# Window attention into a two-layer FFN on one core: the two blocks of a visit multiplied together, queues tied in written order, second-layer weights decoded from the eighth block on

## The chip, the cores and the metric

The kernel runs on one core of a Trainium2 chip. The metric is device time in microseconds from the first to the last instruction, with what lies around them; several runs are taken, and their median counts. PE is the matrix engine, DVE the vector engine, ACT the scalar engine, POOL the GpSimd engine, SP the queue from which all DMA is issued. TensorE's clock has two levels, 1.2 and 2.4 GHz; a granted clock of 1.00 is the higher one all the time.

## The reference

Three stages in a row, all in fp32:

```python
# attention: q, k, v are (4, 8, 576, 64)
scores = (q @ k^T) / sqrt(64), masked to the 64 last positions (0 <= i - j < 64)
x = softmax(scores) @ v                # as (2304, 512): heads side by side
# first layer: w1, w2, w3 are (512, 768), w_out is (768, 512)
x2 = max(x @ w1, x @ w2, x @ w3) @ w_out
# second layer: w_in is (512, 2048), w_out is (2048, 512)
h = x2 @ w_in
g = where(h >= 1, h, where(h <= -1, 0, (h + 1)**2 / 4))
out = g @ w_out                        # (2304, 512)
```

## The kernel before

Every large product is made of three passes: weights and inputs are split into a high half that the matmul takes and a low remainder (high times high, and the two mixed products). The weights come as 64-bit words and are decoded on the chip, 128 x 512 of them at a time, which the text calls a tile: `w_load` issues the DMA (L142), and `w_split` (L154) works on ACT (L165 and a copy, both in place on `wst`), then DVE (a shift, L169, and an add, L170, into `wt`), then ACT (the high half into the slot) and POOL (the remainder, L111). Four `wst` buffers (`NW`) and two `wt` buffers (`WT`) stand in a ring. The loads of q and k for later blocks (`raw`, L208) use the same `wst` ring.

Attention goes by blocks of 64 queries with a window of 128 keys, 36 blocks in all. The stages of a block g are `load`, `vload`, `prep` (transposes of q and k; on DVE from block 16 on, L261), `qk` (scores into `sps2`, L288, then DVE's masked reductions to the maximum, L293), `ex` (ACT's exponentials, L304), `norm` (DVE and POOL), `ptr` and `ptc` (PE transposes and the ACT copy `pt`) and `pv` (value products into `ops2`, L342, an ACT copy and a DVE subtraction into `xt`). `sps2` and `ops2` each hold two blocks, by g % 2, in the same PSUM banks.

The first layer goes by nine blocks of 256 tokens (`blocks1`). A first-step item (`a_item`, L351) is 12 matmuls of 256 columns for one of three weights and one of six columns; an ACT copy or a DVE maximum into `ht` takes it out of PSUM, and after the third weight ACT and POOL make the two halves of `h`. A second-step item (`b_item`, L380) is 18 matmuls, an ACT copy to `x2s` (two buffers) and a store to DRAM on SP. Products, second-layer products and the transposes of q and k share three PSUM buffers (`pmm`).

The order is written by hand in units: an `a_item` is one unit, a `b_item` 1.5, `begin[j]` is where block j starts, and `put` sets every stage at a position. The second step of a block follows the first six items of the next one (`BD`). From block 8 of the attention on, two blocks are done in one visit, a visit every 12 units (`VISITS`, `VSTEP`): a visit holds the value products of one pair, the transposes of the next pair and the scores of the pair after that. Visits start at unit 18. From there on `chained` (L549) ties PE's instructions in the written order; the instructions of the other engines are ordered by a scheduler, which works at build time.

At the end of the attention (0.1 units ahead of the ninth block: the turn), the attention's memory is closed, and `x2t`, more weight slots (`v0` to `v7`) and accumulators (`pacc`) are opened there. The 32 tiles of the second layer (`order2`: w_in and w_out in turn) go to `v0` to `v7` and then to the first layer's slots `u0` to `u23` as they come free. Four are issued at the turn and two with each step of the first 16 of the second layer; the scheduler may move their steps earlier where buffers allow. The second layer goes by blocks of 512 tokens: `c_mm` (12 matmuls, L541), `c_act` (ACT and DVE), and `d_item` (12 matmuls into four accumulators, L606) three steps behind.

## Time and profile before

| what | value |
|---|---|
| median of 3 runs (lowest, highest) | 863.98 us (861.62, 864.16) |
| the profiled execution: its time, its span | 864.39 us, 862.3 us |
| PE busy, share of the span | 798.3 us, 93% |
| DVE, ACT, POOL busy | 363.9, 356.2, 157.9 us |
| share of PE in the chain that ended last | 77% (DVE 5%, DMA 4%, ACT 4%) |
| mean granted clock | 0.985 |

The profiled execution's 864.39 us are its span and 2.1 us around it; it lies 0.41 us above the median. A busy PE is not PE at its peak, since matmuls are pipelined and their ends are modelled. By place, the program is: attention and first layer under the loading and decoding of the first weights to about 90 us, attention and first layer together to about 395 us, the turn to about 458 us, the second layer to the end.

### The profile page before, as it was taken

The page shows a single profiled execution, that of the slowest core. Times are in us where ns is not written, and L with a number is a line of the kernel's source. Part 1 is how long each engine was busy: PE and PEld are TensorE (multiplying, and loading weights), DVE is VectorE, ACT ScalarE, POOL GpSimd, SP SyncE. Part 2 cuts the span into 40 slices and gives each one's busy share as a digit, 9 for nine tenths or more (in the row PEclk, how much of TensorE's full clock was granted, in tenths as well). Part 3 has the DMA queues.
Part 4 walks back from the last instruction along what each step waited for, and adds up shares of the span by engine and source line. Part 5 has one row for each costly group of instructions (what it writes and reads, how often), then busy time and mean ns, then how long its engine had stood idle before and what let it go on. Part 6 is the DMA issues. An engine that isn't in the chain of part 4 may idle for free.

```text
span 862.3 us, 14835 instructions
## 1 busy us (share of the span) xinstructions
PE 798.3 (93%) x5776; PEld 701.6 (81%) x5776; DVE 363.9 (42%) x937; ACT 356.2 (41%) x871; POOL 157.9 (18%) x157
## 2 busy tenths in 40 slices
PE   6698889999999898999779999999999999999998
PEld 4597778889898888898778888888888888888896
DVE  5778422323333432316678733433343334333343
ACT  6988533333333534324779422322232223222232
POOL 3666311111111121213574200000000000000000
PEclk8899999999999999999989999999999999999999
DMA  9976243233141413003777000100020001000000
GB/s 243 279 216 187 43 84 85 52 70 63 40 80 32 135 26 98 14 26 111 234 222 241 24 1 25 62 0 1 1 74 0 1 1 36 25 1 1 24 26 25
DMA packets 128054, 62.70 MB, mean 73 GB/s; under 512 B 98288, under 2 KB 120816, under 8 KB 127984
## 3 DMA queue, kind: packets, MB, share of 16 engines
q1 hardware_dynamic: 127984, 61.76, 26.2%
q8 instruction: 45, 0.74, 0.4%
q14 instruction: 25, 0.20, 0.1%
HBM read 52.30 MB, written 9.44 MB: 72 GB/s over the span
## 4 chain that ended last, share of the span: by engine, by line
PE 77%; DVE 5%; DMA 4%; ACT 4%; issue 2%; SPq 1%; POOL 1%; DVEq 0%; ACTq 0%; POOLq 0%
PE acc L606 23%; PE hp L541 23%; PE ps L363 18%; PE ps L385 7%; DMA wst<-in_moe_w_in 3%; PE ops L342 2%; PE sps L288 2%; PE pps L324 1%; DVE sm L293 1%; SPq L215 1%; DVE wt L170 1%; DMA x2r<-x_scratch 1%; ACT wst L165 1%; DVE wt L169 1%; ACT wst L108 1%
## 5 line engine op out<-in xcount | busy, mean ns | idle before, releaser
L363 PE MATMUL ps<-xt,u 128*128 128x256 f32 x1944 | 239.1, 283 | 9.1 <-DVE ht L372 4.0
L363 PEld LDWEIGHTS ps<-xt,u 128*128 128x128 f32 x1944 | 232.5, 190 | 13.9 <-DVE ht L372 5.2
L541 PE MATMUL hp<-x2t,u 128*128 128x512 f32 (+1 forms) x720 | 161.6, 372 | 0.0
L606 PE MATMUL acc<-u,g 128*128 128x512 f32 x648 | 160.4, 396 | 0.0
L586 ACT ACTIVATE u<-hp,half 128x512 f32<-128x512 f32 (+1 forms) x80 | 51.5, 644 | 251.6 <-PE hp L541 251.5
L541 PEld LDWEIGHTS hp<-x2t,u 128*128 128x128 f32 x720 | 126.9, 188 | 27.2
L606 PEld LDWEIGHTS acc<-u,g 128*128 128x128 f32 x648 | 120.9, 188 | 28.3
L589 DVE SCALAR_TENSOR_TENSOR gt<-u,hp 128x512 f32<-128x512 f32 (+1 forms) x80 | 50.6, 632 | 165.8 <-ACT u L587 165.7
L372 DVE TENSOR_TENSOR ht<-ps,ht 128x256 f32<-128x256 f32 x108 | 45.4, 421 | 131.3 <-PE ps L363 114.0
L385 PE MATMUL ps<-h,u 128*128 128x256 f32 x648 | 82.8, 287 | 4.8 <-ACT h L108 2.4
L385 PEld LDWEIGHTS ps<-h,u 128*128 128x128 f32 x648 | 79.7, 194 | 7.2 <-ACT h L108 2.6
L111 POOL TENSOR_TENSOR u<-wt,u 128x512 fp32r<-128x512 f32 x48 | 67.5, 1408 | 46.7 <-ACT u L108 44.3
L111 POOL TENSOR_TENSOR h<-ht,h 128x256 fp32r<-128x256 f32 x54 | 42.7, 793 | 129.0 <-ACT h L108 128.7
L315 POOL TENSOR_TENSOR sm<-sm,rs 128x512 f32<-128x512 f32 (+1 forms) x36 | 35.8, 994 | 142.4 <-DVE rs L314 130.3
L304 ACT ACTIVATE sm<-sm,nm 128x128 f32<-128x128 f32 (+1 forms) x144 | 55.2, 388 | 15.2 <-DVE nm L293 15.2
L170 DVE CUSTOM_DVE_ANT_0 wt<-wst,wt 128x1024 uint16<-128x1024 uint16 x56 | 56.2, 1004 | 3.5 <-ACT wst L108 0.6
L108 ACT ACTIVATE h<-ht 128x256 fp32r<-128x256 f32 x54 | 22.3, 414 | 83.7 <-DVE ht L372 83.6
L606 PE MATMUL acc<-v,g 128*128 128x512 f32 x216 | 53.6, 394 | 0.0
L541 PE MATMUL hp<-x2t,v 128*128 128x512 f32 (+1 forms) x240 | 53.5, 371 | 0.0
L593 DVE CAST g<-gt 128x512 fp32r<-128x512 f32 (+1 forms) x80 | 34.2, 428 | 45.5 <-PE acc L606 43.1
L111 DVE TENSOR_TENSOR g<-gt,g 128x512 fp32r<-128x512 f32 (+1 forms) x80 | 51.1, 639 | 2.7
L541 PEld LDWEIGHTS hp<-x2t,v 128*128 128x128 f32 x240 | 41.9, 188 | 8.3
(50 smaller groups left out, 627.6 us busy)
## 6 DMA issues: line engine op xcount, KB each, us to landing
wst<-in_moe_w_out SPq DMA_DIRECT2D x22, 512.0 KB, 4.4
wst<-in_moe_w SPq DMA_DIRECT2D x18, 512.0 KB, 5.7
wst<-in_moe_w_in SPq DMA_DIRECT2D x16, 512.0 KB, 4.3
vr<-in_v SPq DMA_DIRECT2D x24, 256.0 KB, 3.0
x_scratch<-x2s SPq DMA_DIRECT2D x36, 128.0 KB, 1.8
out<-ob SPq DMA_DIRECT2D x18, 256.0 KB, 2.0
x2r<-x_scratch SPq DMA_DIRECT2D x16, 256.0 KB, 2.9
vr<-in_v SPq DMA_DIRECT2D x19, 128.0 KB, 3.4
```

What stands on the lines that cost most here:

```text
L111: eng.tensor_tensor(dst, a, b, op=ALU.subtract)
L170: nc.vector.tensor_tensor(t, t, lo, op=ALU.add)
L304: nc.scalar.activation(sm[:, p, 0:W], sm[:, p, 0:W], AF.Exp, bias=d["nm"][:, p:p + 1], scale=-1.0, accum_out=ss[:, p:p + 1])
L315: nc.gpsimd.tensor_tensor(sm[:, :, 0:W], sm[:, :, 0:W], rs.unsqueeze(2).to_broadcast([P, NP, W]), op=ALU.mult)
L363: nc.tensor.matmul(ps[:, 0:n], w_col((w, f), wl, kt), xt[:, xl, kt, 0:n], start=(x == 0), stop=(x == len(passes) - 1))
L372: nc.vector.tensor_tensor(t[:, 0:n], ps[:, 0:n], part[j, f][:, 0:n], op=ALU.max)
L385: nc.tensor.matmul(ps[:, 0:n], w_col((3, f), wl, dt), hts[j, f][:, xl, 0:n], start=(x == 0), stop=(x == len(passes) - 1))
L541: nc.tensor.matmul(ps[:, 0:n], w_col((4, f), wl, kt), x2t[tb][:, xl, kt, 0:n], start=(x == 0), stop=(x == len(passes) - 1),)
L586: nc.scalar.activation(u[:, 0:n], ps[:, 0:n], AF.Relu, bias=half, scale=2.0 ** (-WS / 2 - 1))
L589: nc.vector.scalar_tensor_tensor(gt[:, 0:n], u[:, 0:n], 2.0 ** WS, ps[:, 0:n], op0=ALU.min, op1=ALU.max)
L593: nc.vector.tensor_copy(g[:, 0, 0:n], gt[:, 0:n])
L606: nc.tensor.matmul(accs[t], g[:, gl, t * P:(t + 1) * P], wslot[5, f][:, wl * 512:(wl + 1) * 512], start=(f == 0 and x == 0), stop=(f == KF ...
```

## The change

In a visit, both blocks' value products stand together, and so do both blocks' scores. `pv` keeps the matmuls alone, and `values` copies and subtracts for two blocks at once; `red` takes the reductions out of `qk` and, like `ex`, goes by two of the four head pairs, at positions of its own (`RED`, `EXP`). The second step of the first block follows two items of the second block instead of six. `chained` ties PE, ACT and DVE, each behind its own last instruction, from the first visit on. The second-layer weights have four slots from the start (`V`); loads and decodes are written as two operations, the first four in the eighth block, 16 more from the turn on 1.8 units apart (`W2STEP`), each decode 4.3 units behind its load, and the last 12 beside the second layer.

```diff
--- before.py
+++ after.py
@@ -46,8 +46,15 @@
 VISITS = (-24, -18, -12)
 VSTEP = 12
 VLEAD = 2
-EXP = (1.1, 2.1)
+RED = (0.3, 2.3)
+EXP = (1.7, 3.7)
 PTC = (0.6, 1.6)
+
+
+EW = 4
+W2STEP = 1.8
+W2LAG = 4.3
+W2IN = 20
 
 
 SEQ = (
@@ -118,6 +125,7 @@
     com = ctx.enter_context(tc.tile_pool(name="com", bufs=1))
     stg = ctx.enter_context(tc.tile_pool(name="stg", bufs=2, reuse_waits="tile"))
     U = [com.tile([P, 1024], F32R, name=f"u{i}") for i in range(NU)]
+    V = [com.tile([P, 1024], F32R, name=f"v{i}") for i in range(EW)]
     ident = com.tile([P, P], F32, name="ident")
     half = com.tile([P, 1], F32, name="half")
 
@@ -288,23 +296,29 @@
                     nc.tensor.matmul(
                         sps2[o:o + BL, bank, g % 2, x, 0:W], d["q"][r, p, :], win(r, p), start=True, stop=True
                     )
-
-        for p in range(NP):
+        d.update(sm=sm, nm=nm, W=W)
+
+    def red(g, pairs=range(NP)):
+        d = st_g[g]
+        _, mask, W = window(g)
+        sm, nm = d["sm"], d["nm"]
+
+        for p in pairs:
             nc.vector.tensor_tensor_reduce(
                 out=sm[:, p, 0:W], in0=sps2[:, p // 2, g % 2, p % 2, 0:W], in1=mask, scale=-QSCALE, scalar=BIG,
                 op0=ALU.add, op1=ALU.min, accum_out=nm[:, p:p + 1],
             )
-        d.update(sm=sm, nm=nm, W=W)
-
-    def ex(g):
+
+    def ex(g, pairs=range(NP)):
         d = st_g[g]
         W, sm = d["W"], d["sm"]
-        ss = apool.tile([P, NP], F32, tag="ss", name="ss", bufs=5)
-        for p in range(NP):
+        if pairs[0] == 0:
+            d["ss"] = apool.tile([P, NP], F32, tag="ss", name="ss", bufs=5)
+        ss = d["ss"]
+        for p in pairs:
             nc.scalar.activation(
                 sm[:, p, 0:W], sm[:, p, 0:W], AF.Exp, bias=d["nm"][:, p:p + 1], scale=-1.0, accum_out=ss[:, p:p + 1]
             )
-        d["ss"] = ss
 
     def norm(g):
         d = st_g[g]
@@ -331,7 +345,7 @@
         act_copy(pt[0:W], d["pps"][0:W])
         d["pt"] = pt
 
-    def pv(g, xt, off):
+    def pv(g):
         d = st_g[g]
         W, pt, vr = d["W"], d["pt"], st_g[max(g, 1)]["vr"]
         ops = ops2[:, g % 2]
@@ -342,8 +356,13 @@
                 nc.tensor.matmul(
                     ops[r, p, :], vr[0:W, 2 * p + h, :], pt[0:W, p, o:o + BL], start=True, stop=True
                 )
-        act_copy(xt[:, 0, :, off:off + BL], ops)
-        sub(nc.vector, xt[:, 1, :, off:off + BL], ops, f32(xt[:, 0, :, off:off + BL]))
+
+    def values(g, n, xt, off):
+
+        o = ops2[:, g % 2:g % 2 + n].rearrange("a g p c -> a p g c")
+        hl = [xt[:, x, :, off:off + n * BL].rearrange("a p (g c) -> a p g c", g=n) for x in range(2)]
+        act_copy(hl[0], o)
+        sub(nc.vector, hl[1], o, f32(hl[0]))
 
 
     xts = {}
@@ -427,11 +446,19 @@
         for o in range(0, n, BL):
             gblock[(t0 + o) // BL] = (j, o)
 
-    def pv_x(g):
+    def val(g, n=1):
         j, o = gblock[g]
         if o == 0:
             xt_new(j)
-        pv(g, xts[j], o)
+        values(g, n, xts[j], o)
+
+    def pv_x(g):
+        pv(g)
+        val(g)
+
+    def qk_r(g):
+        qk(g)
+        red(g)
 
 
     order = []
@@ -465,7 +492,8 @@
     late = b_items(0)
     for j in range(1, len(blocks1)):
         items = first if j == 1 else a_items(j)
-        seq += items[:BD] + late + items[BD:]
+        bd = 2 if j == 1 else BD
+        seq += items[:bd] + late + items[bd:]
         late = b_items(j)
     seq += late
     at, begin = 0.0, {}
@@ -482,8 +510,8 @@
         ptr(g)
         ptc(g)
 
-    stages = (load, vload, prep, qk, ex, norm, ptr_c, pv_x)
-    ops0 = dict(L=load, V=vload, P=prep, Q=qk, E=ex, N=norm, T=ptr_c, X=pv_x)
+    stages = (load, vload, prep, qk_r, ex, norm, ptr_c, pv_x)
+    ops0 = dict(L=load, V=vload, P=prep, Q=qk_r, E=ex, N=norm, T=ptr_c, X=pv_x)
     for x, tok in enumerate(SEQ.split()):
         if tok[0] == "W":
             for _ in range(int(tok[1:] or 1)):
@@ -513,23 +541,31 @@
             put(vt, vload, g)
             put(vq + STAGES[2], prep, g)
             put(vq + 0.02, qk, g)
-            put(vq + EXP[y], ex, g)
-            put(vq + EXP[y] + 1, norm, g)
+            for z in range(2):
+                put(vq + RED[y] + z, red, g, (2 * z, 2 * z + 1))
+                put(vq + EXP[y] + z, ex, g, (2 * z, 2 * z + 1))
+            put(vq + EXP[y] + 2, norm, g)
             put(vt + 0.01, ptr, g)
             put(vt + PTC[y], ptc, g)
-            put(vp, pv_x, g)
-    put(begin[len(blocks1) - 1] - 0.1, None)
+            put(vp, pv, g)
+        put(vp + 0.04, val, g1, 2)
 
     order2 = [(w, f) for f in range(KF2) for w in (4, 5)]
-    slots2, w2n = [], [0]
-
-    def w2_next():
-        n = w2n[0]
-        if n < len(order2):
-            w, f = order2[n]
-            st = w_load((w, f), wi2 if w == 4 else wo2, slots2[n], "col" if w == 4 else "row", f)
-            w_split((w, f), st, nc.gpsimd)
-            w2n[0] += 1
+    slots2, staged = list(V), {}
+
+    def w2_load(n):
+        w, f = order2[n]
+        staged[n] = w_load((w, f), wi2 if w == 4 else wo2, slots2[n], "col" if w == 4 else "row", f)
+
+    def w2_split(n):
+        w_split(order2[n], staged.pop(n), nc.gpsimd)
+
+    turn = begin[len(blocks1) - 1]
+    put(turn - 0.1, None)
+    for n in range(W2IN):
+        at = begin[len(blocks1) - 2] + 1 + 4 * n if n < EW else turn + 0.35 + W2STEP * (n - EW)
+        put(at, w2_load, n)
+        put(at + W2LAG, w2_split, n)
 
     hps = {}
 
@@ -544,36 +580,35 @@
             )
 
     order.sort(key=lambda e: e[:2])
-    tail = [None]
-
-    def chained(fn, *args):
-
-        if tail[0] is None:
+    tails = defaultdict(list)
+
+    def chained(fn, *args, tie=True):
+
+        ends = {}
+        with ExitStack() as stack:
+            for i in [i for e in tails for i in tails[e]] if tie else ():
+                stack.enter_context(tc.issue_after(i))
+            n = len(nc.cur_bb.bb.instructions)
             fn(*args)
-        else:
-            with tc.issue_after(tail[0]):
-                fn(*args)
-        pe = [i for i in nc.cur_bb.bb.instructions[-200:] if i.engine == mybir.EngineType.PE]
-        if pe:
-            tail[0] = pe[-1]
-
+        for i in nc.cur_bb.bb.instructions[n:]:
+            if i.engine in TIED:
+                ends[i.engine] = i
+        for e, i in ends.items():
+            tails[e] = [i] if tie else tails[e] + [i]
+
+    TIED = (mybir.EngineType.PE, mybir.EngineType.Activation, mybir.EngineType.DVE)
     for at, _, fn, args in order:
         if fn:
             if (fn, args) == (b_item, (len(blocks1) - 1, 0)):
-                c_mm(0, 0, pacc, "acc")
-            if at < visits[0]:
-                fn(*args)
-            else:
-                chained(fn, *args)
+                chained(c_mm, 0, 0, pacc, "acc")
+            chained(fn, *args, tie=at >= visits[0])
         else:
             att_stack.close()
             p2 = ctx.enter_context(tc.tile_pool(name="p2", bufs=1, side="right", reuse_waits="tile"))
             pacc = ctx.enter_context(tc.tile_pool(name="pacc", bufs=5, space=PSUM))
-            slots2 += [p2.tile([P, 1024], F32R, name=f"v{i}") for i in range(2 * KF2 - NU)] + U
+            slots2 += [p2.tile([P, 1024], F32R, name=f"v{i}") for i in range(EW, 2 * KF2 - NU)] + U
             for kt in range(KD):
                 x2_split(0, p2, kt)
-            for _ in range(4):
-                w2_next()
     ffn_stack.close()
     gp = ctx.enter_context(tc.tile_pool(name="gp", bufs=1, reuse_waits="tile"))
     gts = {}
@@ -623,8 +658,11 @@
             d_item(*seq[x - DLAG])
         c_act(tb, f)
         if tb == 0:
-            w2_next()
-            w2_next()
+            for n in (2 * f, 2 * f + 1):
+                if W2IN + n < len(order2):
+                    w2_load(W2IN + n)
+                if n >= 2 and W2IN + n - 2 < len(order2):
+                    w2_split(W2IN + n - 2)
         if tb + 1 < len(blocks2):
             pl = gp if (tb + 1) % 2 else p2
             if 8 <= f < 8 + KD:
```

PE in the visit of blocks 16 and 17's scores, before and after, with the semaphores that a row waits for (`ops2` are value products, `pps` transposes, `sps2` scores, the number behind a name is that of its buffer; one row is the first matmul of a group, or the rest of it). Before:

```order
L342 MATMUL ops2_103<-pt_1780,vr_1737 64x64 [waits DMAHW5_49,DMAHW4_49]
L342 MATMUL ops2_103<-pt_1780,vr_1737 64x64 x7
L342 MATMUL ops2_103<-pt_1805,vr_1740 64x64 [waits DMAHW3_49,DVE_49]
L342 MATMUL ops2_103<-pt_1805,vr_1740 64x64 x7
L324 MATMUL pps_2013<-ident_85,sm_1752 128x128 [waits PE_49]
L324 MATMUL pps_2013<-ident_85,sm_1752 128x128 x3
L324 MATMUL pps_2018<-ident_85,sm_1766 128x128 [waits PE_49,Pool_49]
L324 MATMUL pps_2018<-ident_85,sm_1766 128x128 x3
L288 MATMUL sps2_102<-kring_101,qt_1938 64x128 x8
L288 MATMUL sps2_102<-kring_101,qt_1941 64x128 [waits DVE_49]
L288 MATMUL sps2_102<-kring_101,qt_1941 64x128 x7
```

After:

```order
L356 MATMUL ops2_107<-pt_1774,vr_1735 64x64 [waits DMAHW5_49,DMAHW4_49]
L356 MATMUL ops2_107<-pt_1774,vr_1735 64x64 x7
L356 MATMUL ops2_107<-pt_1796,vr_1738 64x64 [waits DMAHW4_49]
L356 MATMUL ops2_107<-pt_1796,vr_1738 64x64 x7
L338 MATMUL pps_2008<-ident_89,sm_1750 128x128 [waits PE_49,Pool_49]
L338 MATMUL pps_2008<-ident_89,sm_1750 128x128 x3
L338 MATMUL pps_2013<-ident_89,sm_1760 128x128 [waits PE_49,Pool_49]
L338 MATMUL pps_2013<-ident_89,sm_1760 128x128 x3
L296 MATMUL sps2_106<-kring_105,qt_1938 64x128 [waits DVE_49]
L296 MATMUL sps2_106<-kring_105,qt_1938 64x128 x7
L296 MATMUL sps2_106<-kring_105,qt_1941 64x128 [waits DVE_49]
L296 MATMUL sps2_106<-kring_105,qt_1941 64x128 x7
```

The matmuls stand in the same places. The second block's value products wait for a DMA alone; the DVE waits at the scores are now those for the transposes of q and k (`prep`), one for each block, which stand about three units earlier in DVE's queue.

ACT in the same visit (`x2s` second step, `xt` values, `pt` the transposes' copy, `sm` exponentials, `ht` and `h` first step). Before:

```order
L108 ACTIVATE x2s<-ps 128x256 x3
L108 ACTIVATE xt<-ops_103 128x4x64 x2
L108 ACTIVATE pt<-pps 128x512 x2
L304 ACTIVATE sm,ss<-sm,nm 128x128 x8
L108 ACTIVATE x2s<-ps 128x256
L108 ACTIVATE ht_2095<-ps 128x256
L108 ACTIVATE h<-ht_2172 128x256
```

After:

```order
L115 ACTIVATE x2s<-ps 128x256 x3
L115 ACTIVATE xt<-ops_107 128x4x128
L115 ACTIVATE x2s<-ps 128x256
L115 ACTIVATE pt<-pps 128x512 x2
L319 ACTIVATE sm,ss<-sm,nm 128x128 x2
L115 ACTIVATE ht_2087<-ps 128x256
L319 ACTIVATE sm,ss<-sm,nm 128x128 x4
L115 ACTIVATE h<-ht_2164 128x256
L319 ACTIVATE sm,ss<-sm,nm 128x128 x2
```

The eight exponentials stood in a row; now they stand in twos and fours, with the copies out of PSUM between them.

ACT in the turn, where the decoded tiles are those of `u3` to `u5` (two rows on one `wst` are the two first steps of a tile, `u` is its last ACT step; `wt_5966` was made from `wst_5964`, and after the change `wt_5603` from `wst_5502`, `wt_5642` from `wst_5544`). Before:

```order
L165 ACTIVATE wst_5964<-wst_5964 128x512
L108 ACTIVATE wst_5964<-wst_5964 128x512
L108 ACTIVATE ht0_5479<-ps_5466 128x256
L108 ACTIVATE u3_64<-wt_5915 128x512
L165 ACTIVATE wst_6006<-wst_6006 128x512
L108 ACTIVATE wst_6006<-wst_6006 128x512
L108 ACTIVATE u4_65<-wt_5957 128x512
L165 ACTIVATE wst_6015<-wst_6015 128x512
L108 ACTIVATE wst_6015<-wst_6015 128x512
L108 ACTIVATE h_5511<-ht1_5509 128x256
L108 ACTIVATE ht0_5527<-ps_5514 128x256
L108 ACTIVATE u5_66<-wt_5966 128x512
```

After:

```order
L173 ACTIVATE wst_5502<-wst_5502 128x512
L115 ACTIVATE wst_5502<-wst_5502 128x512
L115 ACTIVATE u3_64<-wt_5603 128x512
L115 ACTIVATE ht0_5623<-ps_5610 128x256
L173 ACTIVATE wst_5544<-wst_5544 128x512
L115 ACTIVATE wst_5544<-wst_5544 128x512
L115 ACTIVATE u4_65<-wt_5642 128x512
L115 ACTIVATE h_5664<-ht1_5662 128x256
L173 ACTIVATE wst_5583<-wst_5583 128x512
L115 ACTIVATE wst_5583<-wst_5583 128x512
L115 ACTIVATE u5_66<-wt_5669 128x512
```

Before, the last step of a tile stood two tiles behind its first steps; now all three stand in a row, and the first layer's copies stand between whole tiles.

## Rows read from the trace of the kernel before

**Rows 1.** The table by windows of 20 us: the stretch and its length, then busy us (and number) of PE matmuls, PE weight loads, DVE, ACT and POOL, the granted clock as a share of full speed, DMA share and GB/s. A steady stretch of the first layer, the turn to the second layer, and the second layer.

```profile
120.00:140.00 20.00, 18.00 (x196) 17.09 (x195) 6.87 (x31) 7.87 (x27) 4.67 (x6) 1.00 0.45 83
...
440.00:460.00 20.00, 16.52 (x104) 15.51 (x105) 13.19 (x21) 16.05 (x32) 12.47 (x10) 0.83 0.71 221
...
480.00:500.00 20.00, 20.00 (x88) 16.14 (x87) 11.38 (x19) 5.76 (x10) 3.62 (x3) 1.00 0.00 1
```

**Rows 2.** The view of who waited for whom, 100 to 380 us: engine and line, what it waited for, us in total, times, longest.

```profile
PE sps L288 <- DVE nm L293: 12.4, 12, 1.1
PE ops L342 <- DVE xt L111: 12.2, 13, 0.9
```

**Rows 3.** The timeline of one visit (pairs of query blocks), and at its end the last value products before the turn: start us, us, engine, line, operation, out<-in, count [idle before <- what ended it]. Value products are L342, scores L288.

```profile
144.77 0.69 PE L342 MATMUL ops<-pt,vr 128*64 128x64 f32 x16
145.92 0.42 DVE L111 TENSOR_TENSOR xt<-ops,xt 128x256 fp32r<-128x256 f32 x1 [6.86 <-ACT xt L108]
146.40 0.69 PE L342 MATMUL ops<-pt,vr 128*64 128x64 f32 x16 [0.94 <-DVE xt L111]
149.76 0.67 PE L288 MATMUL sps<-kring,qt 64*64 64x128 f32 x16 [1.06 <-DVE nm L293]
...
394.67 0.69 PE L342 MATMUL ops<-pt,vr 128*64 128x64 f32 x16 [0.94 <-DVE xt L111]
```

**Rows 4.** The timelines of PE, ACT and SP over the first three visits, same columns.

```profile
76.97 0.46 PE L288 MATMUL sps<-kring,qt 64*64 64x64 f32 x16 [2.21 <-DVE nm L293]
89.71 0.67 PE L288 MATMUL sps<-kring,qt 64*64 64x128 f32 x16 [1.07 <-DVE nm L293]
102.16 0.68 PE L342 MATMUL ops<-pt,vr 64*64 64x64 f32 x16 [0.94 <-DVE xt L111]
105.52 0.67 PE L288 MATMUL sps<-kring,qt 64*64 64x128 f32 x16 [1.05 <-DVE nm L293]
117.66 1.09 PE L249 MATMUL tp<-ident,nat 128*128 128x128 f32 x8 [2.18 <-ACT x2s L108]
...
117.22 0.38 ACT L108 ACTIVATE x2s<-ps 128x256 f32<-128x256 f32 x1 [5.48 <-DMA x_scratch<-x2s]
...
79.52 3.68 SPq L215 DMA_DIRECT2D raw<-in_q  x7
84.36 13.96 SPq L215 DMA_DIRECT2D raw<-in_q  x25
98.42 5.12 SPq L215 DMA_DIRECT2D raw<-in_k  x11
103.63 1.58 SPq L390 DMA_DIRECT2D x_scratch<-x2s  x1
```

**Rows 5.** The timeline of PE at a stop in the sixth block.

```profile
297.48 2.72 PE L363 MATMUL ps<-xt,u 128*128 128x256 f32 x21 [1.23 <-ACT ht L108]
```

**Rows 6.** The timeline of PE around the turn (L363 first step, L385 second step, L541 and L606 second layer), and of ACT at the copy of the last piece of x2.

```profile
377.55 15.56 PE L363 MATMUL ps<-xt,u 128*128 128x256 f32 x132
...
395.28 5.86 PE L363 MATMUL ps<-xt,u 128*128 128x256 f32 x48
...
448.18 0.80 PE L385 MATMUL ps<-h,u 128*128 128x256 f32 x2 [2.37 <-ACT h L108]
449.37 9.16 PE L385 MATMUL ps<-h,u 128*128 128x256 f32 x55 [0.39 <-POOL h L111]
458.36 8.36 PE L541 MATMUL hp<-x2t,v 128*128 128x512 f32 x36
466.56 2.92 PE L606 MATMUL acc<-v,g 128*128 128x512 f32 x12
...
407.14 0.62 ACT L108 ACTIVATE x2t<-x2r 128x512 fp32r<-128x512 f32 x1
```

**Rows 7.** The chain that ended last, in order of time: start us, us, what; three products of the second step.

```profile
366.05 6.29 PE ps L385 x54
```

**Rows 8.** Part 5 of the page: the exponentials, with busy us, mean ns of one, idle before.

```profile
L304 ACT ACTIVATE sm<-sm,nm 128x128 f32<-128x128 f32 (+1 forms) x144 | 55.2, 388 | 15.2 <-DVE nm L293 15.2
```

**Rows 9.** The timelines of ACT, DVE and POOL in the turn: the decode of second-layer weights (ACT L165, L108 on wst, DVE shift L169 and add L170, ACT copy and POOL remainder to u and v).

```profile
427.84 0.66 ACT L165 ACTIVATE wst<-wst 128x512 f32<-128x512 f32 x1
429.95 0.63 ACT L108 ACTIVATE u<-wt 128x512 fp32r<-128x512 f32 x1 [0.90 <-DVE wt L170]
430.49 0.67 ACT L165 ACTIVATE wst<-wst 128x512 f32<-128x512 f32 x1
...
416.51 1.54 DVE L169 TENSOR_SCALAR wt<-wst 128x512 int32<-128x512 int32 x1 [1.19 <-POOL v L111]
421.02 0.43 DVE L169 TENSOR_SCALAR wt<-wst 128x512 int32<-128x512 int32 x1 [1.18 <-POOL u L111]
421.48 0.69 DVE L170 CUSTOM_DVE_ANT_0 wt<-wst,wt 128x1024 uint16<-128x1024 uint16 x1
428.24 1.68 DVE L170 CUSTOM_DVE_ANT_0 wt<-wst,wt 128x1024 uint16<-128x1024 uint16 x1
...
414.74 3.03 POOL L111 TENSOR_TENSOR v<-wt,v 128x512 fp32r<-128x512 f32 x2
428.01 1.36 POOL L111 TENSOR_TENSOR u<-wt,u 128x512 fp32r<-128x512 f32 x1 [0.60 <-ACT u L108]
...
432.31 0.73 POOL L111 TENSOR_TENSOR h<-ht,h 128x256 fp32r<-128x256 f32 x1
```

## The prediction, as it was made before the changed kernel ran

> **What bounds the kernel now.** I read the busy time by stretch first. In a steady stretch of the first layer PE works 18.00 of 20 us, at the turn from the first layer to the second 16.52 of 20 with a granted clock of 0.83, and in the second layer 20.00 of 20 [rows 1]. So PE is the bound everywhere, the second layer has nothing to give, and what can be won are PE's standing times before about 458 us.
>
> The waits of the first layer come next [rows 2]: PE stood 13 times for DVE at the value products, 12.2 us in all, and 12 times at the scores, 12.4 us. One visit in order of time [rows 3] shows why. The value products of one block run, PE stands 0.94 us until DVE has taken the low half of that block (it starts at 145.92), and only then come the next block's. At the scores PE stands 1.06 us for DVE's reductions. That is 2.0 us a visit, and at 144 to 150 us nothing else holds PE.
>
> Before that, in the first three visits, PE stands 2.21, 1.07, 0.94 and 1.05 us for the same reasons and 2.18 us for an x2s copy; ACT had stood 5.48 us for a store of that tile, because SP issues its stores between long rows of loads of q and k [rows 4]. A smaller loss is 1.23 us at 297.48, for an ACT copy [rows 5], while ACT decodes second-layer weights between its own first-layer work.
>
> The turn [rows 6]: the ninth block's first product starts at 396.7 (the 48 matmuls from 395.28, less one item of 12; 132 matmuls take 15.49 us, so an item is 1.41). The first output product of the second layer starts at 466.56, 69.9 us later. Between them lie 18 items (25.4), 8 second-step products of 2.10 [rows 7] (16.8) and four hidden products (36 matmuls take 8.20, so 4 x 2.73 = 10.9): 53.1 us of work, **16.8 us lost**. Part of that is clock: after 2.37 us of standing, 55 matmuls took 9.16 us [rows 6], where the item's rate gives 6.5.
>
> **The change part by part.**
>
> *Products of a visit together, reductions and copies behind them.* No matmul is added. In the order of the changed kernel the second block's value products and scores no longer wait for DVE's work on the first one. From the fourth visit on that frees 13 waits of 0.94 (12 of the 13 in [rows 2], and that of 394.67 [rows 3]) and 11 of 1.06: **23.6 us**. The two copies to xt become one of double width, as do the subtractions. DVE's first reduction now starts after both blocks' scores, 0.67 us later; nobody waits for it until the next visit's transposes, some 20 us on. I cost that at nothing. The cover that could go is in the PSUM ring of three: a product's buffer must be freed within two items, 2.8 us. The order puts exponentials in twos (2 x 0.39 [rows 8]) between evacuations, so nothing should stand that long. If one exponential per visit stuck out, 13 x 0.39 = 5 us would go; that is the low end, 18.6.
>
> *Tied order from unit 18 and the block-0 second step four items earlier.* In the first visits there are 7.45 us of PE standing [rows 4]. Not all of it can go: stores still stand behind loads of q and k on SP, the first behind 48 raw loads of about 0.45 us instead of 43 (7, 25 and 11 before 103.63 [rows 4]). And the products whose copies need the stores now come four items, 5.6 us, sooner. So ACT stands at the third x2s copy again, and its queue is tied behind it. Against that, the decode of the weights whose buffers the raw loads take over now precedes the first exponentials, which lets the row start some 3 us earlier. I take **3 us**, between -3 and 7.4.
>
> *Decoding no longer slipped early into ACT's queue.* The stop of 1.23 us at 297.48 [rows 5] goes; the four tiles that are now decoded in the eighth block, in buffers of their own, are issued on SP right behind the stores of two blocks before, so their data should be there. **1.2 us**, between -1 and 1.2 (four chains of 2.65 us on ACT stand within the 2.8 us of slack, if nothing else does).
>
> *The turn.* 16 tiles are left in it, each 1.8 units (2.5 us) apart on paper, with 12 more after it. Before, the scheduler interleaved the decodes: on ACT the two first steps of a tile were followed by the last step of an older one, 2.65 us from tile to tile (427.84 to 430.49 [rows 9]). Now the queues are tied in written order and each tile's chain runs alone: two ACT steps, shift and add on DVE, a copy on ACT. The shift alone takes 0.43 us, but 1.54 when POOL is in the previous tile's remainder: it started at 416.51 and ended 0.28 after POOL's row did (417.77) [rows 9]. In the serial chain POOL's 1.36 us always start with the next tile's first step, so the shift ends at about 1.7 us, the add (0.69) at 2.4, the copy (0.63) at 3.0. In five of eleven cycles POOL also has an h part of 0.73; I count half of it. That makes 3.15 us a tile. The fifth tile cannot start before the four pieces of x2 are copied, 10.5 us after the ninth block's start (407.14 [rows 6]). Eleven tiles stand before the last item's h in ACT's queue: 10.5 + 34.7 = 45.2. With h and its POOL part the first of the last four products ends near 47, the others 6.3 later, two hidden products 5.5: the output products start at 58.8 instead of 69.9, with 50.4 us of work (one hidden product less ahead of them). Lost: 8.4 instead of 16.8, so **8.4 us** won. Ends: at 2.65 a tile 13.9 won; with shift 1.54 and add 1.68 [rows 9] in every tile 4.3 a tile, 4 lost.
>
> The Trainium skill, SBUF — State Buffer, section Who interferes with whom, has VectorE and GpSimd share a port pair as an exclusive lock that is held for a whole instruction. By that rule the h part on POOL holds up the add in full, 0.38 us more in five tiles, 2 us in all, and the total would be 830; where the lock also falls on the add in the other tiles, it is the second rival below. The trace bears it out for the shift (ended 0.28 us behind POOL) and for some adds (1.68 beside 0.69), not for all.
>
> The clock was granted at 0.83, a mix of 1.2 and 2.4 GHz, after PE had stood in the turn [rows 1, 6]. My turn still has 8 us of standing, in shorter pieces, and I count no drop; one like the old one costs 2.7 us.
>
> *Sum:* 23.6 + 3 + 1.2 + 8.4 = 36.2 off the profiled execution's 864.39 us, 828.2. That execution lies 0.4 above the median of 863.98, so I say **828 us**. The second layer's start, where DVE and ACT still decode 12 tiles beside the new work, I cost at nothing: at 466 us PE ran there unbroken beside the same decode.
>
> **Rivals.**
>
> *Evacuation stuck behind the visit (slower).* Tied queues put products' evacuations behind the softmax in ACT's queue. If all eight exponentials (3.1 us [rows 8]) stood between a finished product and its free buffer, 13 visits cost 40 us and the kernel ends at 868. It decides from 2.8 us a visit (36.2/13). For it: ACT can no longer be reordered. Against: the order has evacuations between the pairs, and two buffers of slack.
>
> *The turn stays bound by the decode chain.* If POOL holds up shift and add in most tiles, a tile takes 3.7 to 4.3 us, and the turn gives 2 or loses 4: 834 to 840. For it: DVE's long rows beside POOL [rows 9]; and it has no slack, since ACT leads in the turn. Against: POOL is busy in only half of each tile. This is the lock of the page named above.
>
> *The turn is covered.* At 2.65 a tile, with all 7.4 us of the early visits, another 9.9: 818. For it: the shift is short whenever POOL is out of the way.
>
> *The change does not do it.* If the second block's matmuls still waited (both lie in the same PSUM tiles), 23.6 us stay: 851. Against: the order names no wait for DVE there, but for the transposes.
>
> **Numbers.** Forecast 0.58 (822 to 833); turn bound by its chain 0.22; turn covered 0.13; waits stay 0.03; slower 0.04. Leaving out the last two and the tails, the range is 816 to 846. About 0.3%, 2.6 us, can be told from no change. Faster by more than that 0.95, within 0.01, slower 0.04.
>
> **What would show it.** Right: PE busy near 20 of 20 between 130 and 380 us; no wait of value products or scores for DVE; the ninth block's start some 28 us earlier; about 3.1 us from tile to tile on ACT in the turn, PE standing some 8 us. Wrong: new PE waits for ACT's ht or x2s copies in each visit; a turn as long as before; PE standing at the start of the second layer; a first visit later than 118 us.

## The result, and the profile after

The changed kernel took **831.36 us** (median; 830.53 to 832.36) beside 862.8 us of the kernel before in the same comparison: a ratio of 0.964, 95% interval 0.961 to 0.966. Forecast were 828 us and 816 to 846. The profiled execution's span is 830.0 us, against 862.3 before.

The visits first: PE's timeline of one visit, then the stretches by 20 us (columns as in [rows 1]).

```profile
146.22 1.15 PE L356 MATMUL ops<-pt,vr 128*64 128x64 f32 x32
147.30 1.09 PE L338 MATMUL pps<-ident,sm 128*128 128x128 f32 x8
148.32 1.10 PE L296 MATMUL sps<-kring,qt 64*64 64x128 f32 x32
```

```profile
60.00:80.00 20.00, 16.20 (x144) 15.26 (x143) 16.39 (x22) 13.96 (x28) 12.57 (x10) 0.91 0.79 226
80.00:100.00 20.00, 13.34 (x106) 12.14 (x107) 9.21 (x35) 12.01 (x37) 8.17 (x8) 0.83 0.31 57
...
120.00:140.00 20.00, 20.00 (x218) 19.46 (x217) 6.73 (x29) 7.90 (x27) 5.98 (x7) 1.00 0.42 75
...
400.00:420.00 20.00, 16.80 (x125) 15.46 (x124) 9.43 (x17) 11.89 (x24) 9.40 (x9) 1.00 0.47 140
```

The value products of both blocks are one row of 32, and so are the scores; nothing stands in brackets behind them. From 100 to 360 us PE is busy 20.00 of 20 us in every stretch, where it was 15.83 to 19.06, mostly 18.00, and the view of who waited for whom has no row for PE there, where [rows 2] had two of 12 us. What is left lies at both ends: 60 to 100 us, with a clock of 0.91 and 0.83 (before: 0.91 and 1.00), and 380 to 440 us.

Three marks that every kernel here has cut the time into stages: the start of the fourth visit's value products (122.89 before, 126.79 after), the start of the last visit's value products (393.04 and 367.22), and the end.

| us | to the fourth visit | fourth to last visit | last visit to the end | span |
|---|---|---|---|---|
| before | 122.89 | 270.15 | 469.26 | 862.3 |
| after | 126.79 | 240.43 | 462.78 | 830.0 |
| saved | -3.90 | 29.72 | 6.48 | 32.3 |
| forecast | 3 | 23.9 | 9.3 | 36.2 |

The forecast's 23.6, 1.2 and 8.4 are put into the same stages here; one stop of 0.94, that of the last visit, counts in the third. So the sum was nearly right while none of its three parts was: the visits gave more, the start lost where a gain was expected, and the last stage gave less. The experiments take the three apart. The table goes on with them (spans of the profiled executions; the medians are of all runs; ratios are to the kernel before, with their 95% intervals):

| kernel | to fourth visit | fourth to last | last to end | span | median | ratio |
|---|---|---|---|---|---|---|
| e1 order of the visit put back | 139.78 | 273.11 | 463.1 | 876.0 | 875.14 | 1.016 (1.013 to 1.018) |
| e2 tied late, six items | 120.71 | 241.17 | 463.6 | 825.5 | 827.17 | 0.958 (0.956 to 0.960) |
| e3 tied late | 117.00 | 240.43 | 463.2 | 820.6 | 822.11 | 0.953 (0.951 to 0.955) |
| e4 turn's decodes in two | 126.61 | 240.43 | 457.9 | 824.9 | 826.34 | 0.957 (0.956 to 0.959) |
| e5 = e3 and e4 | 117.16 | 240.43 | 456.7 | 814.3 | 816.18 | 0.946 (0.945 to 0.948) |
| e6 remainder on DVE | 124.44 | 240.43 | 463.7 | 828.6 | 832.05 | 0.965 (0.963 to 0.966) |
| e7 only PE tied | 116.77 | 249.04 | 468.7 | 834.5 | 836.20 | 0.969 (0.967 to 0.971) |
| e8 first decodes in two | 124.02 | 240.43 | 462.8 | 827.2 | 829.72 | 0.962 (0.960 to 0.963) |
| e9 first softmax early | 126.08 | 240.43 | 461.8 | 828.3 | 830.69 | 0.964 (0.962 to 0.965) |
| e10 = e3 and e1 | 122.80 | 272.45 | 462.9 | 858.2 | 860.40 | 0.998 (0.997 to 0.999) |
| e11 no early tiles | 127.02 | 240.43 | 459.5 | 826.9 | 830.44 | 0.963 (0.961 to 0.965) |
| the changed kernel again | 126.17 | 240.43 | 462.1 | 828.7 | 831.15 | 0.964 (0.963 to 0.966) |

The five kernels whose first visits are written as in the change (it, twice, e4, e6 and e11) came to the fourth visit at 124.4 to 127.0 us, so single profiles differ by 2.6 us there; the middle stage repeats to 0.01 us.

### The profile page after: what moved, and what is told of

Its sections match the earlier page's. It is cut to its first block, busy times and chain, and to the rows that moved or that the text cites. A ratio compares the mean times of both kernels' runs of the same rounds, so it can differ in the third digit from the quotient of the medians.

```text
span 830.0 us, 14782 instructions
## 1 busy us (share of the span) xinstructions
PE 792.4 (95%) x5776; PEld 701.0 (84%) x5776; DVE 356.1 (43%) x923; ACT 349.4 (42%) x857; POOL 156.2 (19%) x157
## 4 chain that ended last, share of the span: by engine, by line
PE 81%; DVE 4%; ACT 3%; issue 2%; DMA 2%; POOL 1%; DVEq 0%; ACTq 0%; POOLq 0%
PE acc L641 24%; PE hp L577 23%; PE ps L382 21%; PE ps L404 7%; DVE wt L178 2%; PE ops L356 2%; PE pps L338 2%; PE sps L296 2%; DVE wt L177 2%; ACT wst L173 1%; DMA x2r<-x_scratch 1%; ACT u L115 1%; POOL u L118 1%; DMA wst<-in_moe_w_out 0%; DMA wst<-in_moe_w_in 0%
## 5 line engine op out<-in xcount | busy, mean ns | idle before, releaser
L404 PE MATMUL ps<-h,u 128*128 128x256 f32 x648 | 79.9, 281 | 2.3 <-POOL h L118 1.2
L404 PEld LDWEIGHTS ps<-h,u 128*128 128x128 f32 x648 | 77.1, 188 | 4.1 <-POOL h L118 1.4
L177 DVE TENSOR_SCALAR wt<-wst 128x512 int32<-128x512 int32 x56 | 37.2, 667 | 42.3 <-ACT wst L173 23.1
L178 DVE CUSTOM_DVE_ANT_0 wt<-wst,wt 128x1024 uint16<-128x1024 uint16 x56 | 49.3, 882 | 5.4 <-ACT wst L115 0.2
```

The lines of the kernel that those rows point to most:

```text
L177: nc.vector.tensor_scalar(t, hi, 3, None, op0=ALU.logical_shift_left)
L178: nc.vector.tensor_tensor(t, t, lo, op=ALU.add)
L404: nc.tensor.matmul(ps[:, 0:n], w_col((3, f), wl, dt), hts[j, f][:, xl, 0:n], start=(x == 0), stop=(x == len(passes) - 1))
```

## The experiments

### e1 and e10: what is a stop worth?

The order of the visit is put back, in e1 with all ties of the change, in e10 with the late tie of e3.

```diff
-            put(vq + 0.02, qk, g)
+            put(vq + 0.02, qk_r, g)
...
-                put(vq + RED[y] + z, red, g, (2 * z, 2 * z + 1))
...
-            put(vp, pv, g)
-        put(vp + 0.04, val, g1, 2)
+            put(vp, pv_x, g)
```

> The changed kernel with the order of a visit put back: each block's reductions stand right behind its scores, each block's copy to xt and subtraction right behind its value products; ties, early tiles and the turn stay. Theory A (a stop costs what the starts show): in the traces a pair of value products takes 2.10 us to the scores' start instead of 3.27, the pair of scores 1.10 instead of 2.39, so 13 x 1.17 + 11 x 1.29 = 29.4 us come back after the third visit, some 3 more before it: 861 to 864. Theory B (a stop costs its idle column, 0.94 and 1.06, as the prediction counted): 23.6 us and 3 before: 855 to 858. Theory C (the ties removed the waits, not the order of the visit): 831.

It took 875.14 us, more than any theory said. The middle stage alone came out near theory A, 273.11 instead of 240.43: of these 32.7 us, 12 stops of 1.17 and 11 of 1.29 make 28.2 and one long stop 3.2 more. The rest went at the start, where the fourth visit came 13 us later than after the change. Theory C is out. PE's timeline in e1, and one row of ACT, say where:

```profile
81.03 0.71 PE L296 MATMUL sps<-kring,qt 64*64 64x64 f32 x16 [6.53 <-DVE nm L307]
...
116.12 1.12 PE L356 MATMUL ops<-pt,vr 64*64 64x64 f32 x16 [3.72 <-DVE xt L118]
...
392.18 1.06 PE L356 MATMUL ops<-pt,vr 128*64 128x64 f32 x16 [4.14 <-DVE xt L118]
...
114.95 0.38 ACT L115 ACTIVATE x2s<-ps 128x256 f32<-128x256 f32 x1 [3.31 <-DMA x_scratch<-x2s]
```

In tied queues, the second half of a pair waits for a DVE step which itself stands behind other work: 6.53 us behind decodes (2.21 before, [rows 4]), 3.72 us since the copy to `xt` stands in ACT's queue behind an x2s copy that waits 3.31 us for a store (0.94 before), and 4.14 in the eighth block, behind such a copy (2.78 us at 388.52) and the decode of an early tile. Behind the second stop the row is long, too (1.12 us where 0.69 is usual): the clock was granted at 0.76 between 80 and 120 us. So the experiment was repeated without ties of ACT and DVE in the first visits:

> The late tie (ACT and DVE tied from the fourth visit on, 822.1 us) with the order of a visit put back, as in the first experiment, whose steady visits gave 32.7 us but whose first visits were disturbed by the ties. Theory A (a stop costs what the starts show, 1.17 at the value products and 1.29 at the scores): 13 x 1.17 + 11 x 1.29 = 29.4, some 3.7 for the three first visits and 3 for the one visit in the eighth block whose copy stands behind a decode: 856 to 860. Theory B (the idle column, 0.94 and 1.06): 850 to 853.

860.40 us, 38.3 more than e3: theory A at its upper edge (856 to 860), and not B. It is also within 0.2% of the kernel before: without the order of the visit, all other parts of the change, tied late, are worth 1.7 us together (860.40 beside 862.08 in the same comparison). One visit of e10:

```profile
122.80 0.69 PE L356 MATMUL ops<-pt,vr 128*64 128x64 f32 x16
124.43 0.69 PE L356 MATMUL ops<-pt,vr 128*64 128x64 f32 x16 [0.94 <-DVE xt L118]
126.07 0.67 PE L296 MATMUL sps<-kring,qt 64*64 64x128 f32 x16
127.79 0.67 PE L296 MATMUL sps<-kring,qt 64*64 64x128 f32 x16 [1.05 <-DVE nm L307]
```

From the first value products to the scores it is 3.27 us here, 2.10 in the changed kernel (146.22 to 148.32). The idle column has 0.94 of that 1.17; the rest, 0.23, is in the busy column: twice 16 matmuls take 2 x 0.69 us, 32 in a row 1.15 (where a row ends is modelled; the sum by starts does not depend on it). At the scores the same sum, 1.05 and twice 0.67 against 1.10, gives 1.29. e10's middle stage is 32.0 us longer than e3's; 12 x 1.17 and 11 x 1.29 make 28.2 of it, and one stop of 4.01 instead of 0.94, in the eighth block as in e1, 3.1; behind that stop the clock was 0.91 from 360 to 380 us, and eight transposes took 1.97 us instead of 1.09. By the idle columns it would be 12 x 0.94 + 11 x 1.06 + 3.1 = 26.0. The stop at the last visit's value products costs nothing that shows: the last stage is 462.9 us in e10 and 463.2 in e3.

### e3, e2, e8 and e9: why the first visits came later

```diff
-            for i in [i for e in tails for i in tails[e]] if tie else ():
+            for i in [i for e in (TIED[:1] if loose else TIED) for i in tails[e]] if tie else ():
...
-            tails[e] = [i] if tie else tails[e] + [i]
+            tails[e] = [i] if tie and not (loose and e != TIED[0]) else tails[e] + [i]
...
-            chained(fn, *args, tie=at >= visits[0])
+            chained(fn, *args, tie=at >= visits[0], loose=at < visits[3])
```

> The changed kernel with ACT and DVE tied only from the fourth visit on; the order of visits, two items ahead of the second step and the turn stay, and so does PE's order. Theory A (decodes whole in the tied queue hold up the first visits): PE's standing between 60 and 125 us falls from 10.5 to the some 4 us that the kernel before had besides its visit waits, and the time to 825 (823 to 827). Theory B (the second step's earlier place): 831, the standing stays.

822.11 us, 0.9 below theory A's range: the tie of ACT and DVE in the first three visits cost 9.3 us, more than the 6 that the standing alone gave (10.5 us after the change, 4.4 in e3), since the clock stayed up as well. Both kernels between 75 and 80 us, the changed one first (POOL's remainders, DVE's shift, ACT, and then rows of PE around that time):

```profile
75.39 2.86 POOL L118 TENSOR_TENSOR u<-wt,u 128x512 fp32r<-128x512 f32 x2
77.03 1.51 DVE L177 TENSOR_SCALAR wt<-wst 128x512 int32<-128x512 int32 x1 [1.20 <-POOL u L118]
79.31 0.63 ACT L115 ACTIVATE u<-wt 128x512 fp32r<-128x512 f32 x1 [2.80 <-DVE wt L178]
...
86.70 5.94 PE L382 MATMUL ps<-xt,u 128*128 128x256 f32 x36 [2.20 <-DVE ht L391]
95.80 0.63 PE L338 MATMUL pps<-ident,sm 128*64 128x128 f32 x4 [2.72 <-POOL sm L329]
```

```profile
76.31 2.55 POOL L118 TENSOR_TENSOR u<-wt,u 128x512 fp32r<-128x512 f32 x2 [0.55 <-ACT u L115]
77.65 1.50 DVE L177 TENSOR_SCALAR wt<-wst 128x512 int32<-128x512 int32 x1
76.92 0.39 ACT L319 ACTIVATE sm<-sm,nm 128x128 f32<-128x128 f32 x1
79.13 0.36 ACT L115 ACTIVATE ht<-ps 128x256 f32<-128x256 f32 x1
...
68.90 4.48 PE L382 MATMUL ps<-xt,u 128*128 128x256 f32 x36 [1.92 <-DVE ht L391]
80.00:100.00 20.00, 18.75 (x198) 17.56 (x198) 12.62 (x38) 13.90 (x40) 11.46 (x10) 1.00 0.34 71
```

POOL is in two remainders until 78.25 and 78.86, and DVE's shift ends 0.29 us behind them in both kernels. After the change ACT has the copy of that tile next and stands 2.80 us for it; the evacuations behind it, and PE for them, are late. In e3 the scheduler has put the exponentials into that time. The transposes come at 86.61 there; after the change the second half of them waits for POOL's norm until 95.80. The clock was granted in full from 60 to 100 us in e3. After the change it was 0.83 from 80 to 100 us, and 36 matmuls behind a stop of 2.20 us took 5.94 us; in e3, 36 behind a stop of 1.92 took 4.48. Between 80 and 100 us the clock was 0.74 to 0.84 in all eight profiles with ACT and DVE tied from the first visit on, and 0.96 to 1.00 in e2, e3, e5, e7, e10 and the kernel before. The 0.91 between 60 and 80 us is not the tie's: the kernel before has it too, and the changed kernel's second profile has 1.00 there.

> The changed kernel with ACT and DVE tied only from the fourth visit on (PE still from the first), and the first block's second step again behind six items of the second block instead of two. Theory A (the 10.5 us of standing between 66 and 96 us come from whole decodes of first-layer weights standing in ACT's tied queue): 825, and within 1.5 us of the same late tie with two items. Theory B (they come from the second step's earlier place, whose stores stand behind loads of q and k): 825 here, but 831 with the late tie alone. Theory C (neither): 831 in both.

827.17 us, 5.1 **more** than e3. So the second step's earlier place helps, and no theory had that. With six items the x2s copies wait for their stores again, as in [rows 4]:

```profile
118.09 0.38 ACT L115 ACTIVATE x2s<-ps 128x256 f32<-128x256 f32 x1 [4.94 <-DMA x_scratch<-x2s]
118.53 2.25 PE L382 MATMUL ps<-xt,u 128*128 128x256 f32 x12 [2.24 <-ACT x2s L115]
```

4.94 us of ACT standing for a store, 2.24 of PE behind it, and a clock below 1.00 in the two stretches around it; in e3 and in both profiles of the changed kernel PE has no such stop (ACT waits for a store even so, 3.83 us at 112.96 in the second of them). Six items with ties from the first visit on was not tried.

What in the tied queue holds the first visits was looked for from two sides. In e8, each decode of the first layer has its last step written behind the next tile's first four; in e9 the first visit's softmax is written right behind its scores.

```diff
...
-            w_split((w, f), st, eng)
+            pend.append(((w, f), w_front(st)))
+            while len(pend) > (n + 1 < len(order1)):
+                w_back(*pend.pop(0), eng)
```

> The changed kernel, all ties as changed, with the first layer's decodes also written in two operations, the last step (ACT copy, POOL remainder) behind the next tile's first four; second-layer decodes stay whole. Theory A (whole decodes in the tied queue, of which ACT waits some 1.1 us each for DVE, hold up the first visits): the standing between 66 and 96 us falls by half or more, the clock there stays at the higher level, and the time is 824 to 827. Theory B (the place of reductions and exponentials behind decodes in the tied queues, whole or not, holds them up): 829 to 832.

```diff
-                put(vq + RED[y] + z, red, g, (2 * z, 2 * z + 1))
-                put(vq + EXP[y] + z, ex, g, (2 * z, 2 * z + 1))
-            put(vq + EXP[y] + 2, norm, g)
+                put(vq + (RED[y] + z if x else 0.03), red, g, (2 * z, 2 * z + 1))
+                put(vq + (EXP[y] + z if x else 0.04), ex, g, (2 * z, 2 * z + 1))
+            put(vq + (EXP[y] + 2 if x else 0.05), norm, g)
```

> The changed kernel, all ties as changed; only in the first visit the reductions, exponentials and norms are written right behind the scores, ahead of the decodes that stand there (u21 to u23). Theory A (the first visits are late because the tied queues put the softmax behind decodes; whole or in two operations makes little difference): the transposes come as early as with the late tie (87 us instead of 92.5 and 95.8), the standing between 66 and 96 us falls to 3 to 6 us, and the time to 823 to 826. Theory B (the decodes' own pace, with POOL behind it, holds up the first-step copies, wherever the softmax stands): the time stays at 829 to 832.

829.72 and 830.69 us: both are theory B, within 2 us of the change. In e9 the wait has only moved:

```profile
80.64 0.63 ACT L115 ACTIVATE u<-wt 128x512 fp32r<-128x512 f32 x1 [2.77 <-DVE wt L178]
81.59 1.68 PE L382 MATMUL ps<-xt,u 128*128 128x256 f32 x12 [2.50 <-ACT ht L115]
86.89 1.71 PE L257 MATMUL tp<-ident,nat 128*128 128x128 f32 x8 [3.61 <-DVE ht L391]
```

ACT stands 2.77 us for the same tile, and PE 2.50 and 3.61 for `ht`, with the exponentials behind the tile instead of among others. Neither fixed order gets round the tile that waits for POOL; a queue that was free to take other work did. Which order would do it with ties is open. It is not shown, either, which of the two ties costs the time, since e3 loosens ACT and DVE together, and no run took POOL's remainder out of this stretch.

### e4, e6 and e11: what bounds the turn

```diff
...
-        put(at + W2LAG, w2_split, n)
+        put(at + W2LAG, w2_front, n)
+        put(at + W2LAG + (1 if n < EW else W2STEP + 0.01), w2_back, n)
```

> The changed kernel with each decode of the first 20 second-layer tiles written as two operations, the last step of a tile (ACT copy, POOL remainder) one tile behind its first four (two on ACT, two on DVE). Theory A (the turn is bound by the serial chain of a tile, 3.15 us from tile to tile on ACT, of which ACT waits 1.1 for DVE): the cycle falls to 2.5 us, the spacing in which they are written, the turn's 8.1 us of standing and the 2.6 behind it fall to 2 to 4, and the time to 823 to 826. Theory B (POOL's remainder, which holds up the shift, sets the cycle): the shift still waits for POOL, the cycle stays near 3 and the time within 2 us of 831. Theory C (wst buffers or DMA set it): ACT waits for loads, 831.

826.34 us, theory A (0.3 above its range): 5.0 saved, all of it in the last stage. The changed kernel's turn, ACT, DVE, POOL and PE, and then e4's:

```profile
387.99 0.67 ACT L173 ACTIVATE wst<-wst 128x512 f32<-128x512 f32 x1
390.33 0.63 ACT L115 ACTIVATE v<-wt 128x512 fp32r<-128x512 f32 x1 [1.12 <-DVE wt L178]
391.13 0.66 ACT L173 ACTIVATE wst<-wst 128x512 f32<-128x512 f32 x1
...
388.75 0.73 DVE L177 TENSOR_SCALAR wt<-wst 128x512 int32<-128x512 int32 x1 [1.60 <-ACT wst L173]
399.05 1.01 DVE L178 CUSTOM_DVE_ANT_0 wt<-wst,wt 128x1024 uint16<-128x1024 uint16 x1
...
387.89 1.29 POOL L118 TENSOR_TENSOR v<-wt,v 128x512 fp32r<-128x512 f32 x1 [1.85 <-ACT v L115]
398.58 0.93 POOL L118 TENSOR_TENSOR h<-ht,h 128x256 fp32r<-128x256 f32 x1
...
391.29 1.69 PE L382 MATMUL ps<-xt,u 128*128 128x256 f32 x12 [1.11 <-ACT x2s L115]
394.43 5.86 PE L382 MATMUL ps<-xt,u 128*128 128x256 f32 x48 [1.45 <-ACT ht L115]
428.21 2.02 PE L641 MATMUL acc<-v,g 128*128 128x512 f32 x8
436.52 5.87 PE L577 MATMUL hp<-x2t,u 128*128 128x512 f32 x24 [2.63 <-DVE gt L624]
```

```profile
383.56 0.67 ACT L175 ACTIVATE wst<-wst 128x512 f32<-128x512 f32 x1
384.67 0.63 ACT L115 ACTIVATE v<-wt 128x512 fp32r<-128x512 f32 x1
385.71 0.68 ACT L175 ACTIVATE wst<-wst 128x512 f32<-128x512 f32 x1
...
387.28 16.16 PE L388 MATMUL ps<-xt,u 128*128 128x256 f32 x132
```

After the change it is 3.14 us from tile to tile (387.99 to 391.13), and ACT stands 1.12 of it for DVE at the copy; in e4 it is 2.15 (1.90 to 2.92 where tiles follow one another), the copy of the tile before follows at once, and PE goes through 132 matmuls from 387.28 without a stop, where it had 1.11, 1.45, 0.16 and 1.04.

```diff
-        w_split(order2[n], staged.pop(n), nc.gpsimd)
+        w_split(order2[n], staged.pop(n), nc.vector if EW <= n < W2IN else nc.gpsimd)
```

> The changed kernel, with the remainder of the 16 tiles of the turn made by DVE instead of POOL; decodes stay whole, ties stay. Theory A (POOL's remainder of the tile before holds up DVE's shift, and that makes the 3.15 us cycle): the shifts in the turn take 0.43 us instead of some 1.5, the cycle falls to some 2.7, PE's 8.1 us of standing in the turn to some 4, and the time to 826 to 828. Theory B (the shift is long for another reason): shifts stay above 1 us, and with 0.65 us more on DVE the time is 831 to 834.

832.05 us: theory B's time with theory A's shifts. There is no gain, and yet POOL does hold DVE up. With POOL's remainders out of the way every shift in the turn takes 0.43 to 0.51 us and every add 0.69, and from copy to copy it is 2.79 us, after the change 3.15:

```profile
385.04 0.63 ACT L115 ACTIVATE v<-wt 128x512 fp32r<-128x512 f32 x1 [0.76 <-DVE wt L178]
387.83 0.63 ACT L115 ACTIVATE v<-wt 128x512 fp32r<-128x512 f32 x1 [0.76 <-DVE wt L178]
...
386.53 0.43 DVE L177 TENSOR_SCALAR wt<-wst 128x512 int32<-128x512 int32 x1
387.10 0.69 DVE L178 CUSTOM_DVE_ANT_0 wt<-wst,wt 128x1024 uint16<-128x1024 uint16 x1
...
PE ps L382 <- DVE ht L391: 2.8, 3, 1.6
```

So POOL's remainder made 0.36 us of the cycle, not the cycle. What was won there was lost again: the maxima of the first step now stand behind the remainder in DVE's queue, and PE stood 2.8 us for them (the last row, of the view of who waited for whom from 355 to 460 us: total, times), where it had 0.2.

```diff
-        at = begin[len(blocks1) - 2] + 1 + 4 * n if n < EW else turn + 0.35 + W2STEP * (n - EW)
+        at = turn + 0.35 + W2STEP * n
```

> The changed kernel, without early tiles: all 20 tiles that stand ahead of the second layer are loaded and decoded in the turn, still 1.8 units apart and whole. Theory A (the turn is bound by the serial chain): four tiles more cost their cycle of 3.15 us each, less the 1.8 units that PE's items take anyway if they slip beside the second layer: PE's standing grows by 8 to 12.6 us, 839 to 844. Theory B (the turn has slack for decoding, and its standing comes from other waits): 831 to 834.

830.44 us: close to theory B's time (831 to 834), and the four tiles decoded in the eighth block are worth nothing that could be measured. But theory B's reason does not hold either, since PE's stops in the turn are those of the change. What is missing in e11 is the stop of 2.63 us for `gt` behind the turn: the last stage of its profile is 459.5 us, that of the changed kernel's two 462.8 and 462.1. The medians show 0.7 to 0.9 us less, within the spread of the runs, and no run shows why the stop went. ACT, and the stretch with the second layer's start:

```profile
390.21 0.63 ACT L115 ACTIVATE v<-wt 128x512 fp32r<-128x512 f32 x1 [1.14 <-DVE wt L178]
393.35 0.63 ACT L115 ACTIVATE v<-wt 128x512 fp32r<-128x512 f32 x1 [1.12 <-DVE wt L178]
...
420.00:440.00 20.00, 20.00 (x100) 16.71 (x99) 17.04 (x26) 16.39 (x31) 6.00 (x5) 1.00 0.71 229
```

The copies of two tiles stand at 390.21 and 393.35; after the change two stood at 390.33 and 393.47. ACT's queue holds the same eleven chains in the turn, those of tiles 1 to 11 instead of 5 to 15, and the other four come beside the second layer, where PE is busy 20.00 of 20 us all the same (17.37 after the change). So what stands in the turn does not go by the number of tiles; that it goes by the spacing of 1.8 units and the chain's length is shown for the chain (e4), not for the spacing, since a wider one was not tried.

### e7 and e5: the ties, and the best of both

```diff
-    TIED = (mybir.EngineType.PE, mybir.EngineType.Activation, mybir.EngineType.DVE)
+    TIED = (mybir.EngineType.PE,)
```

> The changed kernel with PE alone tied in the written order; the scheduler orders ACT and DVE throughout, with all else as changed. Theory A (the order of the visit on PE gives the gain, the ties of ACT and DVE none): steady visits stay without standing, the first visits come as early as with the late tie, and the turn's decodes are interleaved by the scheduler: 815 to 823. Theory B (the ties keep the evacuations in time): PE waits for ACT or DVE appear in the visits, the second-layer decodes slip ahead of first-layer copies as at 297 us of the kernel before, and the time is 826 to 840.

836.20 us, theory B, with theory A right at the start. The visits' second halves wait for nothing (the order on PE does that), and the fourth visit comes at 116.77 as in e3. From there on e7 loses 14.1 us to e3, 8.6 in the middle stage (5.5 of it in the idle column) and 5.5 in the last. Two of PE's stops in the middle, and ACT ahead of them:

```profile
145.97 12.86 PE L382 MATMUL ps<-xt,u 128*128 128x256 f32 x108 [1.46 <-ACT x2s L115]
289.08 0.58 PE L382 MATMUL ps<-xt,u 128*128 128x256 f32 x1 [2.04 <-ACT xt L115]
...
145.17 0.39 ACT L319 ACTIVATE sm<-sm,nm 128x128 f32<-128x128 f32 x1
145.56 0.36 ACT L115 ACTIVATE x2s<-ps 128x256 f32<-128x256 f32 x1
...
287.36 0.65 ACT L173 ACTIVATE wst<-wst 128x512 f32<-128x512 f32 x1 [2.84 <-DMA wst<-in_moe_w_in]
288.45 0.58 ACT L115 ACTIVATE xt<-ops 128x512 fp32r<-128x512 f32 x1
```

The scheduler has all eight exponentials in a row here, from 142.46 to the one shown at 145.17, and the x2s copy behind them: the stop that the prediction's slower rival described, in the kernel that is not tied. At 287.36 a decode has slipped ahead of the copy to `xt` and waits 2.84 us for its load. So the ties of ACT and DVE are worth 14 us from the fourth visit on, and cost 9 before it.

> Both edits that gained: ACT and DVE tied only from the fourth visit on, and the decodes of the first 20 second-layer tiles written in two operations, the second one tile later. The first saved 9.3 us and acts before 125 us, the second 5.0 and acts after 380. Theory A (independent places): 831.4 - 9.3 - 5.0 = 817, between 815 and 819. Theory B (what is gained early is given back at the turn, since the turn is then bound by loads or decoding that do not come earlier): 820 to 822.

816.18 us: the two gains add up (831.36 - 9.3 - 5.0 = 817.1), and this is the fastest version here, 5.4% below the kernel before.

## Why the prediction came out, point by point

- **The order of the visit** was the right mechanism, and its size came from the wrong column. Thirteen waits of 0.94 and eleven of 1.06 are what [rows 2] and [rows 3] put down as idle; by the starts a pair costs 1.17 and 1.29, 29.4 instead of 23.6 (as written, 13 x 0.94 and 11 x 1.06 are 23.9; 23.6 follows from the totals of [rows 2]). Of the 29.4, e10 bears out the 28.2 that lie in the middle stage, not the 1.17 of the last visit. What the short rows of 16 matmuls add was left out; e10 shows it.
- **Evacuations stuck behind exponentials**, the slower rival, did not come: PE waited for nothing between 100 and 352 us. It came where the ties were left out, in two visits and at 1.46 and 1.32 us (e7). Costing the late reductions at nothing held.
- **The first visits** were the step that failed. Forecast were 3 us won, bounded by -3, and 3.9 were lost. The prediction took the visits' standing of 7.45 us [rows 4] as what could go and looked for its danger in the stores. The stores were not it: ACT still waits for one in the changed kernel's second profile, but PE does not, and the earlier second step is worth 5 us (e2). What it did not price was its own sentence about the turn, that a tied decode runs alone, at the place where decodes already stood beside the softmax: the tie there cost 9.3 us (e3), partly as clock. That the tile which waits for POOL is the reason is read from the rows; no run takes it away. "I count no drop" was said of the turn, where it held; the drop came at 80 to 100 us.
- **The stop at 297 us** [rows 5] is gone, as forecast. That early tiles' loads would be in time held too; but they bought nothing (e11). In e7, where the scheduler orders ACT, such a stop is back at 289 us.
- **The turn** was forecast at 58.8 us from the ninth block's start to the first output product. It took 58.5 (369.7, which is 368.30 and one item of 1.41, to 428.21). The tile's 3.15 us, an average with POOL's h parts in it, was 3.14 where a single evacuation stood in the cycle and 3.25 on average (378.56 to 411.05, ten cycles): the copy starts 2.34 us behind the first step instead of 2.4, and the evacuations on ACT, 0.26 us each, were not counted. The chain began 8.9 us behind the block's start instead of 10.5, which makes up for it, so that 58.5 lies this close to 58.8 is in part luck. e4 shows that the serial chain is what bound PE there. What was forecast wrongly is behind it: "the second layer's start ... I cost at nothing" cost a stop of 2.63 us at 436.52, for `gt` of DVE, which the prediction had named as a sign of being wrong; from the first output product to the end it took 401.8 us against 395.7, where the hidden product that now comes later accounts for 2.7. The remaining 0.7 was not traced.
- **The lock of DVE and POOL.** The change's shifts end 0.3 us behind POOL's row (389.48 and 389.18; 78.54 and 78.25) however early they start, and the add at 399.05 ends 0.55 behind the h part (400.06 and 399.51); without POOL they take 0.43 and 0.69 (e6). So DVE loses the overlap, all but some 0.14 us of it. The Trainium skill's rule (SBUF — State Buffer, section Who interferes with whom: an exclusive lock) agrees with these rows, for the adds too, of which the prediction doubted it. In the chain of a tile, though, the overlaps are short and cost 0.3 us each, and the second rival, tiles of 3.7 to 4.3 us, did not come.

The misses had both signs, -6.9 at the start, 5.8 in the visits and -2.8 behind them, so the sum lies nearer to the result than its parts; that is in part luck.

## What to carry to other kernels

Price a stop by the distance between the starts around it, in the row with and the row without it, not by its idle column: the two rows of a short burst that is cut in two add up to more than the one row, and the idle column leaves that out. Tying queues in a written order is worth what the order is worth at each place: here 14 us from the fourth visit on, and minus 9 in the first three, where decodes that wait for a third engine stood ahead of evacuations, so tie by stretches. Before moving work out of a crowded stretch, ask whether its length or only its spacing there bounds the neighbour; four tiles less changed nothing, and writing each tile in two halves gained 5 us.
